# The low parts of the weights: GpSimd in quarters in the first layer, VectorE in the second

## The chip, the cores and the metric

The kernel runs on one core of one Trainium2 chip. The metric is the device time of one execution in microseconds (us). The engines are TensorE (PE; its weight loads are PEld), VectorE (DVE), ScalarE (ACT), GpSimd (POOL) and SyncE (SP), which here issues loads. Each engine works through its own instructions in the order of the program and waits for the others by semaphores.

## What is computed

```python
def reference(q, k, v, moe_*, moe2_*):
    x = attention(q, k, v)          # 4 x 8 heads, 576 tokens, window 32, plain or with dilation 4
    x = x as [2304, 512]
    # first layer: 8 experts with 288 tokens each; the largest logits of x @ w_gate choose first
    for e in range(8):
        out[mask_e] = relu(x[mask_e] @ w1[e]) @ w2[e]        # w1 [512, 1024], w2 [1024, 512]
    # second layer: each token goes to the two best experts of its noisy logits
    for e in range(8):
        out2[mask_e] += weight * (relu(x[mask_e] @ w1b[e]) @ w2b[e])
```

All inputs are float32, and the routing depends on small differences of the logits, so the products have to be nearly as exact as float32.

## The kernel before

The work has three parts: the attention (to about 104 us), the first layer with its routing (to about 500 us) and the second layer (to the end).

**Products in split form.** TensorE multiplies a shorter format (float32r) fast. So each operand is split into a high part, the number rounded to that format, and a low part, the rest; a product is the sum of high x high, high x low and low x high (`mm3`, L688). Weights come in chunks of 128 x 1024: four for an expert's first matrix, four for its second, 64 chunks in each layer. `split` (L662 to L668) makes the parts of one chunk: ScalarE copies `raw` into `whi` (L666), GpSimd subtracts `whi` from `raw` into `wlo` (L667). There are 10 buffers each for `whi` and `wlo` and 4 for `raw`; SyncE's loads run four chunks ahead.

```python
nc.scalar.activation(hi, raw, AF.Copy)
nc.gpsimd.tensor_tensor(lo, raw, hi.bitcast(F32), op=OP.subtract)
```

The other operands are split on ScalarE and VectorE: a token tile from PSUM into `xh` and `xl` (L671, L672), a hidden tile into `hh` and `hl` (L675, L676). The products write into four PSUM buffers `m`; one comes free when its `hl` is done.

**First layer.** `routing` finds, expert by expert, the threshold of the logits digit by digit. A round has three steps on VectorE and two on TensorE: VectorE compares (`I`, L479), TensorE counts (18 narrow products, L495), VectorE marks (`sat`, L497) and makes the next key ready (`wd`, L501), TensorE adds up (L506), VectorE takes the digit off (`w`, L510). `lister` then builds the list of the expert's tokens (L608 to L632), and GpSimd gathers their rows (`gather1`, L698). Between the routing's steps TensorE works on products of the expert before (`ffn1`).

**Between the layers** `noisy` (L804 to L849), `ranks0` and `ranks` work out the second layer's routing on VectorE.

**Second layer.** For each expert, `up` makes the first product on its 640 slots (segments of 256 and 384 columns) and `down` the second, 512 columns wide in five blocks, whose results GpSimd adds to the output rows (L1001). While an expert's first product runs, `slots` (L903 to L940) makes the next expert's list of tokens: VectorE's `rke` (L912), 24 one-hot blocks `R` (L917) and `A` (L924, L926), then 24 narrow products (L931).

**What sets the order.** The program is written out in the order in which it is to run. `build` keeps an estimated TensorE clock, `self.pe`, which each product moves on (`spend`), and puts routing steps, background tasks and splits among the products by it: `SPLITS1`, `SPLITS2` and `SPLITS2F` (L43 to L45) are the times, within an expert's products, at which the next chunk is split.

Of the kernel before, what the change touches and what calls it, by code (L numbers as in the profile page):

```python
# [22 lines left out]
CAP = N // E            # tokens of an expert of the first layer  # L23
NT = N // 128           # 18 token tiles
GB = 96                 # rows of a block of the first layer
NJ = CAP // GB          # 3 blocks
NCOL = E * NJ           # 24 columns of 96 positions
NA = NCOL - 2 * NJ      # those of all but the last two experts
XW = DM + E             # a gathered row: the token and its noise
CB = 5                  # blocks of 128 slots of an expert of the second layer  # L30
CAP2 = CB * 128
SEGS = ((0, 256), (256, 384))
BA = 3                  # blocks of the first expert that do not wait for the last of the first layer
SA = BA * 128
NB = 9                  # query blocks of 64
KW = 96                 # keys of a query block's window
DIGITS = (6, 6, 6, 7, 7)  # bits of the digits of a key
# [4 lines left out]
# times, in an expert's products, at which the next chunk of weights is split  # L42
# [4 lines left out]
LOAD = (3.0, 5.0)       # from a load's start to its arrival: of a known expert, of one that is read first  # L47
ROWS0 = (4, 1, 2, 1, 2, 1, 2, 1, 2, 1, 1)
WARM = (14, 2, 9)
HOP = (0.13, 0.2)       # from the vector to the tensor engine and back  # L50
SLACK = (0.1, 0.4, 0.0, 0.2)

# columns of the constants: those that stay, then those that are only converted
# [89 lines left out]
class Body:  # L143
# [3 lines left out]
    # ------------------------------------------------------------ constants  # L147
# [42 lines left out]
    # ------------------------------------------------------------ attention  # L190
    def attention(self, x0T):
        nc, tc, A = self.nc, self.tc, self.A
        with ExitStack() as ctx:
# [109 lines left out]
            def gate(b):  # L303
                """The four feature chunks' shares of the logits, each in a quarter of the partitions."""
                for o in (b * S, b * S + 288):
                    ps = pT.tile([128, 512], F32, name="ps")
                    for kk in range(4):
                        nc.tensor.matmul(ps[32 * kk:32 * kk + 32, :288], self.wg1[:, kk, :],
                                         x0T[kk][:, o:o + 288], start=True, stop=True)
                    nc.scalar.activation(gs[:, o:o + 288], ps[:, :288], AF.Copy)  # L310
# [15 lines left out]
            # the digits' values, by doubling  # L326
# [5 lines left out]
            def warm(n):  # L332
                """Keeps the tensor engine's clock up while it waits for loads."""
# [23 lines left out]
            for u, (g, j0, n) in enumerate(groups):  # L357
# [16 lines left out]
                if g == 4 and j0 == 0:  # L374
                    # the parts of the rows that the transpositions do not write
                    nc.sync.dma_start(self.xr[:, DM:XW], A["noise"])
                if CLEAR <= u < CLEAR + 9:
                    # zeros to which the second layer adds
# [6 lines left out]
    # ------------------------------------------------------- first routing  # L385
# [12 lines left out]
    def rows(self, x0T, c0, c1, psum, name, pool):  # L398
        """The tokens' rows of features for the gathers."""
# [9 lines left out]
    def routing(self):  # L409
        """Yields (kind, phase, time of the products that follow); an expert is closed in each phase."""  # L410
# [29 lines left out]
        def choices():  # L440
            """Each token's first best expert among the open ones, and order-preserving bits of its value."""
# [13 lines left out]
        def prefix():  # L455
            """Members of EQ before each, by columns."""
# [5 lines left out]
        def place(pk):  # L462
            """Ranks of the members; the others lie far behind."""
# [9 lines left out]
        for k in range(E - 1):  # L473
            ei = self.st.tile([1, 1], I32, name=f"ei{k}")
            self.EV[k] = ei
            # w: above, at or below the threshold's digits so far
# [54 lines left out]
            # the taken tokens leave  # L531
# [7 lines left out]
        # the expert that is left takes every token that has not been taken  # L539
# [24 lines left out]
    def chain(self, t):  # L564
        """The vector engine's time for the routing's next operations."""
# [3 lines left out]
    def shade(self, dur):  # L569
        """Work for the vector engine while the routing waits for products that take dur."""  # L570
# [7 lines left out]
    def later(self, t, f):  # L578
        """f as soon as the routing leaves the vector engine time for it."""
# [14 lines left out]
    def lister(self, k, rk):  # L594
        """The tokens of phase k's expert by their ranks, [96, 3], in pieces of work."""
# [45 lines left out]
    # ------------------------------------------------------------- weights  # L641
    def raw1(self, w1, c, e=None):
        """Rows 128c.. of an expert's first matrix, [512, 1024]."""
# [8 lines left out]
    def raw2(self, w2, c, e=None):  # L652
        """Rows 256c.. of an expert's second matrix, [1024, 512]."""
# [8 lines left out]
    def split(self, raw):  # L662
# [4 lines left out]
        nc.gpsimd.tensor_tensor(lo, raw, hi.bitcast(F32), op=OP.subtract)  # L667
        return hi, lo  # L668
# [10 lines left out]
    def mm3(self, ps, pairs, late=None):  # L679
        """ps = sum of a.T @ b over the pairs of split operands; yields its times."""  # L680
# [11 lines left out]
    # --------------------------------------------------------- first layer  # L692
# [26 lines left out]
    def ffn1(self, k):  # L719
        """Yields (unit name, time on the tensor engine)."""  # L720
# [4 lines left out]
        for f in range(8):  # L725
            ps = self.mm.tile([128, 512], F32, name="m")
            fs = slice(f * 128, (f + 1) * 128)
            yield from self.mm3(ps[:, :CAP], [((self.W[0, k, c][0][:, fs], self.W[0, k, c][1][:, fs]),
                                               (xh[:, c, :], xl[:, c, :])) for c in range(4)])
# [4 lines left out]
        for d in range(4):  # L734
            ps = self.mm.tile([128, 512], F32, name="m")
            pairs = []
            for f in range(8):
                c, a = divmod(f, 2)
                ds = slice(a * DM + d * 128, a * DM + (d + 1) * 128)
                pairs.append(((self.W[1, k, c][0][:, ds], self.W[1, k, c][1][:, ds]), (hh[:, f, :], hl[:, f, :])))  # L740
# [4 lines left out]
    def gate2(self, k):  # L745
        """Products with the second gate, by positions."""
# [16 lines left out]
    def rows1(self, k):  # L763
        """The rows of the first layer's output."""
# [582 lines left out]
```

## Time and profile before

| | us |
|---|---|
| median of 3 runs | 1029.07 |
| lowest and highest run | 1026.8, 1032.75 |
| the profiled execution (its span) | 1035.7 |
| PE, DVE, ACT, POOL busy in it | 944.6, 476.7, 368.5, 488.2 |
| mean granted TensorE clock | 0.905 of full |

The times of the profile are counted from the start of the span. A row of a timeline gives the start, the length, the engine, the line, the operation and the tiles (out<-in); in brackets stands the idle time ahead of it and what ended it. The granted clock is the one that the throttle gave TensorE; 1.0 is 2.4 GHz, 0.5 is 1.2 GHz.

### The profile page before, as it was taken

To read this page: it belongs to the slowest core of one execution; us is meant where nothing else is said; L and a number is where in the kernel's file an instruction comes from. 1 tells how busy PE (TensorE), PEld (TensorE's weight loads), DVE (VectorE), ACT (ScalarE), POOL (GpSimd) and SP (SyncE) were. 2 spreads that over 40 slices of the span, in tenths; PEclk is the share of its full clock that TensorE was granted. 3 is DMA by queue.
4 is the path that set the end of the run, shared out by engine and by line. 5 is a ranking of instruction groups with operands and counts; after the bars stand their busy time and mean duration, and the time that the engine had idled before them with its cause. 6 is when DMAs were issued, how large, how long until landed. Compare 5 with 4: busy or idle time off the path is not lost.

```text
span 1035.7 us, 17494 instructions
## 1 busy us (share of the span) xinstructions
PE 944.6 (91%) x6986; PEld 855.7 (83%) x6988; DVE 476.7 (46%) x1342; ACT 368.5 (36%) x669; POOL 488.2 (47%) x279
## 2 busy tenths in 40 slices
PE   8889947998989999996998989999898998989994
PEld 5677747988979989996997988988888898888983
DVE  6565476577375574238255460522616034160310
ACT  2657322232223234562551423423323343322310
POOL 4654045434425255774643665455454645545311
PEclk8989558788888689997999989999999999989998
DMA  9674452333313233562543445355353533533212
GB/s 301 204 244 140 184 186 87 100 111 99 109 61 121 90 105 126 189 207 84 157 144 72 127 139 132 82 139 97 101 122 92 152 74 113 104 112 92 28 18 38
DMA packets 59643, 126.33 MB, mean 122 GB/s; under 512 B 7456, under 2 KB 14880, under 8 KB 59552
## 3 DMA queue, kind: packets, MB, share of 16 engines
q1 hardware_dynamic: 46080, 94.50, 27.7%
q0 software_dynamic: 10496, 25.77, 13.2%
q10 hardware_dynamic: 2976, 4.85, 1.4%
q8 instruction: 57, 0.93, 0.4%
q14 instruction: 34, 0.28, 0.1%
HBM read 100.46 MB, written 24.72 MB: 121 GB/s over the span
## 4 chain that ended last, share of the span: by engine, by line
PE 70%; DVE 20%; DMA 4%; ACT 2%; issue 2%; POOL 1%; SPq 0%; ACTq 0%; POOLq 0%; DVEq 0%
PE m L688 53%; PE r L495 6%; DVE R L917 4%; DMA kt<-in_k_dram 2%; PE t L963 2%; PE s L236 2%; DVE hl L676 1%; PE o L287 1%; PE t L404 1%; DVE wd L501 1%; DVE rke L912 1%; PE t L712 1%; DMA out_dram<-y,tk 1%; DVE I L479 1%; PE ps L268 1%
## 5 line engine op out<-in xcount | busy, mean ns | idle before, releaser
L667 POOL TENSOR_TENSOR wlo<-raw,whi 128x1024 fp32r<-128x1024 f32 x128 | 319.4, 2513 | 275.0 <-ACT whi L666 261.3
L688 PE MATMUL m<-xh,whi 128*128 128x384 f32 (+2 forms) x768 | 248.0, 323 | 10.9 <-DVE hl L676 10.9
L688 PE MATMUL m<-xl,whi 128*128 128x384 f32 (+2 forms) x768 | 246.2, 321 | 0.0
L688 PE MATMUL m<-xh,wlo 128*128 128x384 f32 (+2 forms) x768 | 245.4, 320 | 0.0
L676 DVE SCALAR_TENSOR_TENSOR hl<-m,hh 128x256 fp32r<-128x256 f32 (+2 forms) x192 | 89.8, 474 | 191.3 <-ACT hh L675 191.2
L675 ACT ACTIVATE hh<-m 128x256 fp32r<-128x256 f32 (+2 forms) x192 | 82.0, 428 | 260.8 <-PE m L688 256.9
L688 PEld LDWEIGHTS m<-xh,whi 128*128 128x128 f32 x768 | 154.5, 201 | 13.0 <-DVE hl L676 12.6
L688 PEld LDWEIGHTS m<-xl,whi 128*128 128x128 f32 x768 | 154.8, 202 | 5.4 <-issue 5.0
L688 PEld LDWEIGHTS m<-xh,wlo 128*128 128x128 f32 x768 | 154.4, 201 | 0.5 <-POOL wlo L667 0.5
L666 ACT ACTIVATE whi<-raw 128x1024 fp32r<-128x1024 f32 x128 | 133.4, 1050 | 8.2 <-DMA raw<-in_w1a_dram 6.4
L688 PE MATMUL m<-whi,hl 128*128 128x512 f32 x320 | 126.0, 394 | 2.6 <-DVE hl L676 2.6
L688 PE MATMUL m<-whi,hh 128*128 128x512 f32 x320 | 128.3, 401 | 0.0
L1001 POOL DMA_INDIRECT out_dram<-y,tk x40 | 63.0, 1576 | 136.3 <-ACT y L1000 79.5
L688 PE MATMUL m<-wlo,hh 128*128 128x512 f32 x320 | 125.4, 392 | 0.0
L672 DVE TENSOR_TENSOR xl<-t,xh 128x512 fp32r<-128x512 f32 (+1 forms) x72 | 42.1, 586 | 169.0 <-ACT xh L671 168.8
L688 PE MATMUL m<-hh,whi 128*128 128x288 f32 x256 | 84.5, 330 | 3.4 <-DVE ge L608 3.4
L688 PE MATMUL m<-hl,whi 128*128 128x288 f32 x256 | 84.9, 332 | 0.0
L495 PEld LDWEIGHTS <-I 128*64 128x64 bf16 (+1 forms) x630 | 63.8, 195 | 25.1 <-DVE I L479 21.0
L688 PE MATMUL m<-hh,wlo 128*128 128x288 f32 x256 | 84.3, 329 | 0.0
L495 PE MATMUL r<-OH,I 128*64 128x8 bf16 (+1 forms) x630 | 66.8, 239 | 18.1 <-DVE I L479 18.1
L1000 ACT ACTIVATE y<-m,wte 128x512 f32<-128x512 f32 x40 | 27.6, 689 | 150.7 <-PE m L688 81.5
L688 PEld LDWEIGHTS m<-whi,hl 128*128 128x128 f32 x320 | 60.4, 189 | 16.1 <-DVE hl L676 3.5
(205 smaller groups left out, 1290.2 us busy)
## 6 DMA issues: line engine op xcount, KB each, us to landing
raw<-in_w1a_dram SPq DMA_DIRECT2D x32, 512.0 KB, 3.8
raw<-in_w2a_dram SPq DMA_DIRECT2D x32, 512.0 KB, 3.3
raw<-in_w1b_dram SPq DMA_DIRECT2D x32, 512.0 KB, 3.3
raw<-in_w2b_dram SPq DMA_DIRECT2D x32, 512.0 KB, 3.3
vt<-in_v_dram SPq DMA_DIRECT2D x8, 768.0 KB, 6.5
qt<-in_q_dram SPq DMA_DIRECT2D x8, 576.0 KB, 8.3
kt<-in_k_dram SPq DMA_DIRECT2D x8, 576.0 KB, 9.0
out_dram<-z SPq DMA_DIRECT2D x9, 512.0 KB, 7.4
```

Of the source, the lines that this page charges most:

```text
L236: nc.tensor.matmul(s[r, i, jj * KW:(jj + 1) * KW], QT[g][r, i, 64 * j:64 * j + 64], KT[g][r, i, w:w + KW], start=True, stop=True)
L495: nc.tensor.matmul(pc[:nb, :E], I[:, :nb, c], OH[:, c, :], start=c == 0, stop=c == NT - 1)
L666: nc.scalar.activation(hi, raw, AF.Copy)
L667: nc.gpsimd.tensor_tensor(lo, raw, hi.bitcast(F32), op=OP.subtract)
L672: self.nc.vector.tensor_tensor(xl, ps, xh.bitcast(F32), op=OP.subtract)
L675: self.nc.scalar.activation(hh, ps, AF.Relu)
L676: self.later(0.4, lambda: self.nc.vector.scalar_tensor_tensor(hl, ps, 0.0, hh.bitcast(F32), op0=OP.max, op1=OP.subtract))
L688: self.nc.tensor.matmul(ps, a, b, start=i == 0, stop=i == n - 1)
L917: V.tensor_scalar(R[:, c, :], self.iotab[:GB], rk[:, c:c + 1], None, op0=OP.is_equal)
L963: nc.tensor.transpose(ps[:, kk * 128:(kk + 1) * 128], g[:, kk * 128:(kk + 1) * 128], self.ident)
L1000: nc.scalar.activation(y, ps, AF.Copy, scale=wt[:, b:b + 1])
L1001: nc.gpsimd.indirect_dma_start(out=self.out, out_offset=bass.IndirectOffsetOnAxis(ap=tok[:, b:b + 1], axis=0), in_=y, in_offset=None, comp ...
```

## The change

In the first layer the low part of a chunk is still subtracted on GpSimd, in four instructions of 256 columns each. In the second layer it is subtracted on VectorE, in one instruction of 1024 columns. That one is not put into the program where the chunk is split, but kept (`pend`) until the estimated TensorE clock has moved on by 2.5, or until a product is about to use the chunk. TensorE's, ScalarE's and SyncE's instructions stay as they were, in the same order.

```diff
-    def split(self, raw):
+    def split(self, chunk, raw):
...
         nc.scalar.activation(hi, raw, AF.Copy)
-        nc.gpsimd.tensor_tensor(lo, raw, hi.bitcast(F32), op=OP.subtract)
-        return hi, lo
+        self.W[chunk] = hi, lo
+        if chunk[1] < E:
+            for q in range(0, F, F // 4):
+                s = slice(q, q + F // 4)
+                nc.gpsimd.tensor_tensor(lo[:, s], raw[:, s], hi[:, s].bitcast(F32), op=OP.subtract)
+        else:
+            self.pend[chunk] = self.pe + 2.5, lambda: nc.vector.tensor_tensor(lo, raw, hi.bitcast(F32), op=OP.subtract)
+
+    def lows(self, t=1e9):
+        for chunk in [c for c, (at, _) in self.pend.items() if at <= t]:
+            self.pend.pop(chunk)[1]()
+
+    def w(self, chunk, s):
...
+        if chunk in self.pend:
+            self.pend.pop(chunk)[1]()
+        hi, lo = self.W[chunk]
+        return hi[:, s], lo[:, s]
...
         def spend(t):
             self.pe += t
+            self.lows(self.pe)
...
-                self.W[chunks[i]] = self.split(raw[i])
+                self.split(chunks[i], raw[i])
```

`ffn1`, `up` and `down` take the parts of a chunk by `self.w(chunk, columns)` instead of from `self.W`.

VectorE, while an expert of the second layer makes its first product and the next expert's slots are worked out. Before (`rke`, `R` and `A` are tiles of `slots`, `hl` the low part of a hidden tile):

```order
L912 SCALAR_TENSOR_TENSOR rke<-a_7603,rke 96x24
L917 TENSOR_SCALAR R_7606<-iotab,rke 96x128 x6
L676 SCALAR_TENSOR_TENSOR hl_7481<-m,hh_7480 128x256
L917 TENSOR_SCALAR R_7606<-iotab,rke 96x128 x12
L676 SCALAR_TENSOR_TENSOR hl_7483<-m,hh_7482 128x384
L917 TENSOR_SCALAR R_7606<-iotab,rke 96x128 x6
L676 SCALAR_TENSOR_TENSOR hl_7481<-m,hh_7480 128x256
L921 TENSOR_TENSOR Ab_7678<-ge_7600 96x120
```

The same place in the change, whose lines from `split` on are numbered 18 or 19 higher:

```order
L930 SCALAR_TENSOR_TENSOR rke<-a_7794,rke 96x24
L935 TENSOR_SCALAR R_7797<-iotab,rke 96x128 x6
L695 SCALAR_TENSOR_TENSOR hl_7673<-m,hh_7672 128x256
L935 TENSOR_SCALAR R_7797<-iotab,rke 96x128 x6
L676 TENSOR_TENSOR wlo<-raw,whi 128x1024
L935 TENSOR_SCALAR R_7797<-iotab,rke 96x128 x6
L695 SCALAR_TENSOR_TENSOR hl_7675<-m,hh_7674 128x384
L935 TENSOR_SCALAR R_7797<-iotab,rke 96x128 x6
L695 SCALAR_TENSOR_TENSOR hl_7673<-m,hh_7672 128x256
L939 TENSOR_TENSOR Ab_7870<-ge_7791 96x120
```

One subtraction has come between the second and the third six of the 24 blocks `R`. The other seven of an expert lie outside these rows: two between the `hl` ahead of the slots, one behind the slots' results and four, in a row, ahead of the five `xl` of the next expert's tokens.

GpSimd, the first chunks of the first layer and the gathers of its first two experts. Before:

```order
L667 TENSOR_TENSOR wlo<-raw,whi 128x1024
L698 DMA g<-xr,idx_1888 96x520 x3
L667 TENSOR_TENSOR wlo<-raw,whi 128x1024 x11
L698 DMA g<-xr,idx_2448 96x520 x3
L667 TENSOR_TENSOR wlo<-raw,whi 128x1024 x5
```

In the change:

```order
L674 TENSOR_TENSOR wlo<-raw,whi 128x256 x4
L717 DMA g<-xr,idx_1891 96x520 x3
L674 TENSOR_TENSOR wlo<-raw,whi 128x256 x44
L717 DMA g<-xr,idx_2484 96x520 x3
L674 TENSOR_TENSOR wlo<-raw,whi 128x256 x20
```

Each subtraction has become four; the gathers stand at the same places among the chunks.

## Rows read from the trace of the kernel before

**Rows 1.** The source line L667: shortest, median and longest in ns; who waited (us, times).
```profile
L667 POOL TENSOR_TENSOR wlo<-raw,whi x128: 2330/2402/2998, 133.5 to 971.5; 128x1024 fp32r<-128x1024 f32 x128
...
  PEld m L688: 0.5, 1
```

**Rows 2.** The source lines L912 and L501, columns as in rows 1.
```profile
L912 DVE SCALAR_TENSOR_TENSOR rke<-a,rke x9: 174/2002/2002, 485.2 to 914.8; 96x24 f32<-96x24 f32 x8, 96x18 f32<-96x18 f32 x1
...
L501 DVE SCALAR_TENSOR_TENSOR wd<-w,dd x27: 162/166/6946, 111.2 to 364.9; 128x18 f32<-128x18 bf16 x27
```

**Rows 3.** Timeline of DVE around 668, within the first product of an expert.
```profile
664.81 0.56 DVE L676 SCALAR_TENSOR_TENSOR hl<-m,hh 128x384 fp32r<-128x384 f32 x1 [1.77 <-ACT hh L675]
...
666.24 2.00 DVE L912 SCALAR_TENSOR_TENSOR rke<-a,rke 96x24 f32<-96x24 f32 x1
668.27 1.06 DVE L917 TENSOR_SCALAR R<-iotab,rke 96x128 bf16<-96x128 bf16 x6
...
669.59 4.20 DVE L917 TENSOR_SCALAR R<-iotab,rke 96x128 bf16<-96x128 bf16 x12
```

**Rows 4.** Timeline of POOL in the same stretch.
```profile
665.80 2.40 POOL L667 TENSOR_TENSOR wlo<-raw,whi 128x1024 fp32r<-128x1024 f32 x1 [4.63 <-ACT whi L666]
```

**Rows 5.** Timeline of PE in the same stretch.
```profile
674.31 0.44 PE L688 MATMUL m<-xh,whi 128*128 128x384 f32 x1 [1.60 <-DVE hl L676]
...
677.01 0.76 PE L931 MATMUL r<-A,R 96*128 96x35 bf16 x24 [1.39 <-DVE A L926]
```

**Rows 6.** The chain that ended last: start, us, what; three of the experts.
```profile
677.77 30.00 PE m L688 x150
...
863.07 31.52 PE m L688 x150
...
926.49 32.19 PE m L688 x150
```

**Rows 7.** Stretches: length, busy PE, PEld, DVE, ACT, POOL; granted clock, DMA share, GB/s.
```profile
127.00:167.00 40.00, 19.79 (x147) 18.11 (x146) 30.16 (x62) 11.26 (x19) 22.28 (x11) 0.63 0.39 134
167.00:395.00 228.00, 216.74 (x1541) 201.69 (x1540) 145.85 (x448) 65.74 (x124) 92.92 (x47) 0.81 0.33 106
456.00:494.00 38.00, 28.89 (x203) 26.99 (x202) 31.33 (x130) 15.27 (x30) 19.65 (x10) 0.82 0.34 115
...
677.00:739.00 62.00, 59.00 (x366) 53.47 (x366) 21.98 (x58) 20.78 (x34) 32.06 (x18) 1.00 0.46 111
```

**Rows 8.** DVE by line and shape: count, busy us, mean ns, idle time before.
```profile
L672 DVE TENSOR_TENSOR xl<-t,xh 128x512 fp32r<-128x512 f32 x40 | 27.6, 691 | 157.7 <-ACT xh L671 157.7
...
L672 DVE TENSOR_TENSOR xl<-t,xh 128x288 fp32r<-128x288 f32 x32 | 14.4, 454 | 11.4 <-ACT xh L671 11.1
```

**Rows 9.** POOL by line and shape, columns as in rows 8.
```profile
L247 POOL TENSOR_TENSOR p<-p,mx 128x960 f32<-128x960 f32 x8 | 14.3, 1792 | 16.1 <-DVE mx L246 15.3 <-PE s L236 0.8
...
L247 POOL TENSOR_TENSOR p<-p,mx 128x768 f32<-128x768 f32 x8 | 11.8, 1470 | 3.1 <-DVE mx L246 2.7 <-PE o L287 0.4
```

**Rows 10.** Timelines of POOL, DVE and PE in the first expert's routing.
```profile
140.48 6.93 POOL L667 TENSOR_TENSOR wlo<-raw,whi 128x1024 fp32r<-128x1024 f32 x3
155.62 9.94 POOL L667 TENSOR_TENSOR wlo<-raw,whi 128x1024 fp32r<-128x1024 f32 x4 [8.21 <-ACT whi L666]
...
140.51 6.95 DVE L501 SCALAR_TENSOR_TENSOR wd<-w,dd 128x18 f32<-128x18 bf16 x1
...
161.28 2.02 DVE L510 TENSOR_SCALAR w<-wd,r 128x18 bf16<-128x18 f32 x1
163.34 3.44 DVE L479 TENSOR_TENSOR I<-thr,w 128x2304 bf16<-128x2304 bf16 x1
...
148.65 1.60 PE L495 MATMUL r<-OH,I 128*64 128x8 bf16 x12 [7.84 <-DVE I L479]
```

**Rows 11.** The chain that ended last: two of its stretched DVE pieces.
```profile
133.75 2.32 DVE dg L486 x2
...
386.75 2.80 DVE idx L631
```

More of the change, by code (lines that the diff above doesn't have):

```diff
@@ L727, in ffn1 @@
             fs = slice(f * 128, (f + 1) * 128)
-            yield from self.mm3(ps[:, :CAP], [((self.W[0, k, c][0][:, fs], self.W[0, k, c][1][:, fs]),
-                                               (xh[:, c, :], xl[:, c, :])) for c in range(4)])
+            yield from self.mm3(ps[:, :CAP], [(self.w((0, k, c), fs), (xh[:, c, :], xl[:, c, :])) for c in range(4)])
             self.split_h(ps[:, :CAP], hh[:, f, :], hl[:, f, :])
@@ L739, in ffn1 @@
                 ds = slice(a * DM + d * 128, a * DM + (d + 1) * 128)
-                pairs.append(((self.W[1, k, c][0][:, ds], self.W[1, k, c][1][:, ds]), (hh[:, f, :], hl[:, f, :])))
+                pairs.append((self.w((1, k, c), ds), (hh[:, f, :], hl[:, f, :])))
             yield from self.mm3(ps[:, :CAP], pairs, 5 if d == 0 else None)
@@ L978, in up @@
                 ps = self.mm.tile([128, 512], F32, name="m")
-                yield from self.mm3(ps[:, :n], [((self.W[0, E + e, c][0][:, fs], self.W[0, E + e, c][1][:, fs]),
-                                                 (xh[:, c, o:o + n], xl[:, c, o:o + n])) for c in range(4)])
+                yield from self.mm3(ps[:, :n], [(self.w((0, E + e, c), fs), (xh[:, c, o:o + n], xl[:, c, o:o + n])) for c in range(4)])
                 self.split_h(ps[:, :n], hh[:, f, :], hl[:, f, :])
@@ L996, in down @@
                 ds = slice(a * DM, (a + 1) * DM)
-                pairs.append(((hh[:, f, bs], hl[:, f, bs]), (self.W[1, E + e, c][0][:, ds], self.W[1, E + e, c][1][:, ds])))
+                pairs.append(((hh[:, f, bs], hl[:, f, bs]), self.w((1, E + e, c), ds)))
             yield from self.mm3(ps, pairs, 5 if b == b0 else None)
@@ L1024, in build @@
         nc.gpsimd.memset(self.cnt, 0.0)
-        self.G1, self.G2, self.X1T, self.XX, self.SL, self.HH, self.W = ({} for _ in range(7))
+        self.G1, self.G2, self.X1T, self.XX, self.SL, self.HH, self.W, self.pend = ({} for _ in range(8))
         self.pe = self.tR = self.dR = self.dv = self.rdy = 0.0
```

## The prediction

> **What bounds the kernel now.** I read the page first: TensorE is busy nine tenths of the span, VectorE and GpSimd less than half, so what can be won is TensorE's idle time behind the attention and the time it spends at its lower clock. Next I read the subtraction that is moved. On GpSimd it takes 2402 ns in the median, and TensorE waited for its result once, for 0.5 us [rows 1]. Its own length is hidden; what matters is what it does to others, and that shows on VectorE. The small instruction of L912 (96x24) takes 174 ns at best and 2002 ns in the median; that of L501 (128x18) takes 166 ns in the median and 6946 ns at worst [rows 2]. In the expert boundary that I looked at, L912 starts at 666.24 and ends at 668.24, just behind the GpSimd subtraction that began at 665.80 and ends at 668.20 [rows 3, 4]. The run of twelve L917 takes 4.20 us, though six take 1.06 [rows 3]; the next subtraction lies across it. So a VectorE instruction that reads two SBUF operands, or goes from SBUF to SBUF, stands still while GpSimd subtracts; those that read PSUM (L676, L672) are not stretched. **The wait for GpSimd to end ends last at these places**, though no semaphore carries it.
>
> TensorE pays for it. In this boundary it stood 1.60 us for an hl of L676, late behind the stretched L917, and 1.39 us for A of L926 [rows 5]: 3.0 us. The same pair stands in five experts (at 672.7, 734.5, 796.2, 858.0 and 921.3), and as much in the first boundary, at 606.6. Another stall stands ahead of 549. Behind some stalls the granted clock is the lower level: the 150 products behind the slots take 30.00 us in one expert, but 31.52 and 32.19 us in two others [rows 6], together 3.7 us more. In the first layer TensorE is idle for 40.00 - 19.79 = 20.2 us between 127 and 167, for 11.3 us between 167 and 395 and for 9.1 us between 456 and 494, at a mean granted clock of 0.63, 0.81 and 0.82 [rows 7].
>
> **The change, second layer.** 64 subtractions leave GpSimd; its gathers and scatters stay. VectorE gets 64. The trace has no such instruction on it; the nearest rows are L672, the same subtraction from PSUM: 691 ns for 512 columns, 454 for 288 [rows 8], so 1.06 ns a column and 149 fixed, **1.23 us** for 1024. The upper bound is GpSimd's 2.40, the lower 1.09, with nothing fixed. Eight per expert make 9.8 us more for VectorE, which was busy for 22 of 62 us [rows 7]. Four lie in the second product, where VectorE has only the five xl to do; two lie between hl, in its pauses, and one behind the slots' results. One lies within the slots, behind the second six of L917. It follows ScalarE's copy by several us, so it does not wait there. Queued behind it are two runs of L917, two hl and A.
>
> The slots' chain, from the hl ahead of it to A, took 12.2 us (664.81 to 677.01 [rows 3, 5]). The locks in it are 2.00 - 0.17 = 1.83 us at L912 and 4.20 - 2.12 = 2.08 us at L917. Less these and plus 1.23 it takes 9.5, and A ends at 674.3. Without the stall for hl (that hl then ends near 671.6, and was asked for at 672.7) TensorE would be there at 677.01 - 1.39 - 1.60 = 674.02 [rows 5]. So 0.3 of 3.0 us remain: 2.7 us for each of six boundaries, **16 us** (9 if one more subtraction falls into the chain, 18 at most). The longer products behind stalls give **3 us** (0 to 3.7). Around 549 two such waits go and up to four subtractions of 1.23 come into the same chain: **0** (-1 to 2).
>
> **The change, first layer.** 64 subtractions become 256. For the price of a quarter: GpSimd's subtractions of 960 and 768 columns take 1792 and 1470 ns [rows 9], so 182 ns are fixed; (2402 - 182) / 4 + 182 = **0.74 us**, at least 0.60 with nothing fixed. Four take 2.95, so a chunk holds GpSimd 0.55 us longer. These 64 x 0.55 = 35 us lie beside TensorE, whose products hardly wait for wlo [rows 1]; if that cover went, each chunk would come 0.55 us late.
>
> What VectorE wins depends on how it gets in. Between whole subtractions it does: GpSimd runs four from 155.62 to 165.56; w, begun at 161.28, ends at 163.30, and I goes from 163.34 to 166.78 [rows 10], held once by each of two subtractions. With quarters an instruction would wait 0.74 us at most instead of 2.4, but the next one may meet the next quarter. In the chain I count fifteen single waits between 133.75 and 386.75, the first and the last in [rows 11], whose instructions are 1.5 to 2.6 us longer than their like, 31 us in all. Bounds for each: 1.4 us won, if the other quarters run while VectorE waits for TensorE; 0.9 lost, if four quarters hit four instructions in turn. VectorE is idle for a good third of 167 to 395 [rows 7], so I take half of the win, 0.7: 10.5 us. The sixteenth wait is another. wd stood from 140.51 to 147.46, through three subtractions (140.48 to 147.41) right behind a gather, and TensorE stood 7.84 us [rows 10]; the last of the fifteen, L631, also began beside a gather and ended with the subtraction behind it. VectorE got in at no joint there. Twelve quarters would hold wd for 12 x 0.74 = 8.9 us, a loss of 1.9. Of 10.5 - 1.9 some 0.7 reaches TensorE (of its 31.5 us idle in 127 to 395 some 26 lie behind the first subtraction; the waits are 38): **6 us** (-11 to 19). In 456 to 494 six instructions were held about as long as L912, but there one instruction follows another without a pause, so each quarter would find a new one: **0** (-4 to 7). For the clock I take **2 us** (0 to 10): the first layer's narrow routing products precede most of its low stretches, and they stay.
>
> The row behind the gather is where the Trainium skill, page "SBUF — State Buffer", section "SBUF: two separate sides", speaks otherwise: the port pair that VectorE and GpSimd share is locked for one whole instruction by whichever begins first. By that rule wd would wait for one quarter and the sum be an estimated 6 us better; by the row it is not. The wait at L912 (2.0 us) agrees with the rule, the one through three subtractions does not.
>
> **Sum.** 16 + 3 + 0 + 6 + 0 + 2 = 27 us. The profiled execution took 1035.7, 6.6 above the median of the runs: 1035.7 - 27 = 1008.7 there, 1029.07 - 27 = **1002 us** for the median. The terms' bounds, added as squares since they go their own ways, are 17 us down and 19 up: 985 to 1021.
>
> **The rivals.**
> *Quarters hold the port as one piece.* If VectorE is let in at no joint between quarters, each of the fifteen waits grows by 0.55 and wd by 1.9, (8.3 + 1.9) x 0.7 = 7 us, and 456 to 494 loses 2 to 3; the second layer's 19 stay: 1029 - 19 + 10 = 1020. For it: wd and L631. Against it: w and I [rows 10]. Chance 0.18. The Trainium skill, page "GPSIMD Engine Reference", section "2.1 Instruction dispatch", has such a mechanism: each of GpSimd's cores goes on to the next instruction when its own share is done. The trace agrees behind gathers alone.
>
> *The subtraction takes the lock's place on VectorE.* If two more of the eight fall ahead of hl and A than the one I count, 1.23 each, the stalls of the second layer stay at 2.7, and only the first layer wins: 1029 - 8 = 1021. For it: VectorE would work some 22 of a first product's 28 us. Against it: the pauses ahead of each hl. That VectorE was not held by GpSimd at all, and the change only moves work, ends at the same place. Chance 0.10.
>
> *Quarters meet VectorE in turn: slower.* If GpSimd takes the port after each VectorE instruction and 2.5 quarters of each chunk hit one, VectorE waits 1.85 us per chunk, where it now waits 0.8 (38 and 12 us over 64 chunks): 64 x 1.05 x 0.7 = 47 us lost against 19 won, 1057. It decides from 64 x 0.7 x d = 19, d = 0.42 us more per chunk: 1.6 quarters. For it: w and I, held one behind the other. Against it: the third of its time in which VectorE waits for TensorE and quarters pass. Chance 0.07.
>
> *All joints free, and the clock with them.* Terms at their upper bounds: 18 + 4 + 2 + 19 + 7 + 10 = 60, 969. Chance 0.06.
>
> **How the numbers follow.** The forecast has the other 0.59. The range, 977 to 1021, holds nearly all of it and most of the first two rivals; the slower and the best case are left out. A measurement of this kernel tells about 0.5%, 5.1 us, from no change: faster is under 1023.9. Of the forecast, the best case and the first two rivals (0.93) I leave 0.07 for same: 0.86 faster, 0.07 same, 0.07 slower.
>
> **What would show it.** Second layer: L912 near 0.18 us, twelve L917 near 2.1 in sum, wlo on VectorE near 1.23 us, TensorE's stall ahead of L931 under 0.5 us, the 150 products 30.0 us in every expert. First layer: quarters of 0.60 to 0.74 us, single waits under 0.8 us, wd of the first expert held for 7 us or more. I am wrong if TensorE still stands 2 us at each expert boundary, if quarters take over 0.8 us, or if the 40 us of idle time between 127 and 494 grow.

## The result, and the profile after

| | before | the change |
|---|---|---|
| median of 4 runs, us | 1028.84 | 995.91 |
| lowest and highest, us | 1026.8, 1032.75 | 990.73, 1000.84 |
| span of the profiled run, us | 1035.7 | 988.9 |
| mean granted TensorE clock in it | 0.905 | 0.924 |

The ratio is 0.9659, with an interval of 0.9627 to 0.969: faster by 33 us, where 27 had been forecast. The spans of the two profiled runs lie on opposite sides of the medians (before 6.9 above, after 7.0 below) and differ by 46.8 us; terms that are read from the two profiles add up to that, not to 33.

The engines on the page of the change: GpSimd is busy for 376.6 us instead of 488.2, VectorE for 497.7 instead of 476.7.

```profile
PE 925.4 (94%) x6988; PEld 839.2 (85%) x6988; DVE 497.7 (50%) x1406; ACT 368.4 (37%) x669; POOL 376.6 (38%) x407
```

The source lines of the change that answer to [rows 1, 2] (shortest, median and longest in ns): the quarter on GpSimd, the subtraction on VectorE, `rke`, and `wd`.

```profile
L674 POOL TENSOR_TENSOR wlo<-raw,whi x256: 712/737/3000, 133.4 to 479.8; 128x256 fp32r<-128x256 f32 x128
...
L676 DVE TENSOR_TENSOR wlo<-raw,whi x64: 1211/1218/1228, 482.4 to 927.7; 128x1024 fp32r<-128x1024 f32 x64
...
L930 DVE SCALAR_TENSOR_TENSOR rke<-a,rke x9: 174/179/181, 465.0 to 873.2; 96x24 f32<-96x24 f32 x8, 96x18 f32<-96x18 f32 x1
...
L501 DVE SCALAR_TENSOR_TENSOR wd<-w,dd x27: 164/166/1669, 110.7 to 352.3; 128x18 f32<-128x18 bf16 x27
```

The two prices that no row of before had were right: 0.74 us a quarter (737 ns), 1.23 us the subtraction on VectorE (1218). `rke`, which took 2002 ns in the median, takes 179. The worst `wd` took 6946 ns and takes 1669.

**Second layer.** VectorE within one expert's first product, which answers to [rows 3]:

```profile
755.44 0.18 DVE L930 SCALAR_TENSOR_TENSOR rke<-a,rke 96x24 f32<-96x24 f32 x1
755.66 1.06 DVE L935 TENSOR_SCALAR R<-iotab,rke 96x128 bf16<-96x128 bf16 x6
...
757.94 1.22 DVE L676 TENSOR_TENSOR wlo<-raw,whi 128x1024 fp32r<-128x1024 f32 x1
...
762.71 0.60 DVE L944 TENSOR_TENSOR A<-Ab,W 96x360 bf16<-96x360 f32 x1
```

TensorE at the end of it, which answers to [rows 5]: the stall of 1.60 us for `hl` is gone, and of the 1.39 us for A 0.40 is left.

```profile
763.36 0.76 PE L949 MATMUL r<-A,R 96*128 96x35 bf16 x24 [0.40 <-DVE A L944]
```

In the chain that ended last, all six pieces of 150 products now take the time of the fast ones in [rows 6]; the first and the last of them:

```profile
587.38 30.00 PE m L707 x150
...
881.90 30.00 PE m L707 x150
```

**First layer.** The stretches of [rows 7] in the change. TensorE is idle for 11.4 us of the first (20.2 before), 10.3 of the second (11.3) and 6.3 of the third (9.1); the granted clock (before it the busy times) is 0.69, 0.84 and 0.91 instead of 0.63, 0.81 and 0.82.

```profile
127.00:167.00 40.00, 28.60 (x211) 26.37 (x211) 27.84 (x93) 12.43 (x22) 27.86 (x35) 0.69 0.45 151
167.00:395.00 228.00, 217.69 (x1587) 203.07 (x1588) 135.89 (x429) 72.49 (x138) 119.94 (x155) 0.84 0.33 108
456.00:494.00 38.00, 31.69 (x250) 30.16 (x249) 23.73 (x61) 16.39 (x27) 17.16 (x24) 0.91 0.48 156
```

These are the same times and not the same work: the first slots' product, in the third stretch, starts at 489.32 before and at 469.10 in the change. From 127 us to that product TensorE does the same 2310 products in both. It is idle meanwhile for 40.7 us before (362.30 - 321.59) and for 29.5 in the change, and busy for 9.0 us less (before, then the change):

```profile
127.00:489.30 362.30, 321.59 (x2310) 302.21 (x2310) 219.18 (x666) 124.03 (x232) 173.45 (x86) 0.82 0.37 121
```

```profile
127.00:469.10 342.10, 312.61 (x2310) 293.50 (x2310) 197.46 (x662) 123.74 (x231) 207.87 (x272) 0.85 0.39 128
```

The biggest single gain there contradicts the forecast. `wd` behind the first gathers was to be held through twelve quarters; the timelines of GpSimd, VectorE and TensorE, which answer to [rows 10], show it through in 0.28 us. TensorE's idle time of 7.84 us became 1.98.

```profile
139.97 8.85 POOL L674 TENSOR_TENSOR wlo<-raw,whi 128x256 fp32r<-128x256 f32 x12
...
139.86 0.28 DVE L501 SCALAR_TENSOR_TENSOR wd<-w,dd 128x18 f32<-128x18 bf16 x1
140.25 0.57 DVE L510 TENSOR_SCALAR w<-wd,r 128x18 bf16<-128x18 f32 x1
140.86 1.22 DVE L479 TENSOR_TENSOR I<-thr,w 128x1152 bf16<-128x1152 bf16 x1
...
142.13 1.12 PE L495 MATMUL r<-OH,I 128*64 128x8 bf16 x8 [1.98 <-DVE I L479]
```

Two things stayed as forecast. `idx`, behind another gather, is held through all four quarters that follow (GpSimd, then VectorE):

```profile
374.30 2.78 POOL L674 TENSOR_TENSOR wlo<-raw,whi 128x256 fp32r<-128x256 f32 x4
...
373.87 3.23 DVE L631 SCALAR_TENSOR_TENSOR idx<-cp 96x3 int32<-96x3 f32 x1
```

And where VectorE has one instruction behind the other, each meets a quarter of its own, so that TensorE's stall there is what it was (6.28 us before). VectorE, then TensorE:

```profile
457.08 0.72 DVE L861 CAST W<-nzs 96x144 bf16<-96x144 f32 x1
457.83 0.68 DVE L862 TENSOR_TENSOR nzs<-nzs,W 96x144 f32<-96x144 f32 x1
...
469.10 0.63 PE L949 MATMUL r<-A,R 96*128 96x21 bf16 x18 [6.31 <-DVE A L944]
```

### The profile page after: what moved, and what is told of

It is laid out like the page before. It is cut to its first block, busy times and chain, and to the rows that moved or that the text cites. A ratio compares the mean times of both kernels' runs of the same rounds, so it can differ in the third digit from the quotient of the medians.

```text
span 988.9 us, 17657 instructions
## 1 busy us (share of the span) xinstructions
PE 925.4 (94%) x6988; PEld 839.2 (85%) x6988; DVE 497.7 (50%) x1406; ACT 368.4 (37%) x669; POOL 376.6 (38%) x407
## 4 chain that ended last, share of the span: by engine, by line
PE 72%; DVE 18%; ACT 3%; issue 3%; DMA 2%; POOL 0%; SPq 0%; ACTq 0%; POOLq 0%; DVEq 0%
PE m L707 53%; PE r L495 6%; DVE R L935 3%; PE s L236 2%; PE t L981 2%; DVE hl L695 2%; DMA kt<-in_k_dram 1%; PE o L287 1%; PE t L404 1%; DVE wlo L676 1%; DVE I L479 1%; PE t L788 1%; PE t L731 1%; PE ps L268 1%; PE t L769 1%
## 5 line engine op out<-in xcount | busy, mean ns | idle before, releaser
L674 POOL TENSOR_TENSOR wlo<-raw,whi 128x256 fp32r<-128x256 f32 x256 | 190.2, 778 | 144.2 <-ACT whi L669 127.5
L707 PE MATMUL m<-xh,whi 128*128 128x384 f32 (+2 forms) x768 | 242.4, 316 | 1.2 <-DVE ge L608 1.2
L707 PE MATMUL m<-xl,whi 128*128 128x384 f32 (+2 forms) x768 | 242.5, 316 | 0.0
L707 PE MATMUL m<-xh,wlo 128*128 128x384 f32 (+2 forms) x768 | 241.1, 314 | 0.0
L1018 POOL DMA_INDIRECT out_dram<-y,tk x40 | 66.3, 1658 | 253.0 <-ACT y L1017 204.8
L707 PEld LDWEIGHTS m<-xl,whi 128*128 128x128 f32 x768 | 151.1, 197 | 4.6 <-issue 4.2
L707 PEld LDWEIGHTS m<-xh,whi 128*128 128x128 f32 x768 | 150.7, 196 | 3.2 <-DVE ge L608 1.5
L707 PEld LDWEIGHTS m<-xh,wlo 128*128 128x128 f32 x768 | 150.3, 196 | 0.5 <-issue 0.5
L669 ACT ACTIVATE whi<-raw 128x1024 fp32r<-128x1024 f32 x128 | 133.5, 1051 | 11.4 <-DMA raw<-in_w1a_dram 8.6
L676 DVE TENSOR_TENSOR wlo<-raw,whi 128x1024 fp32r<-128x1024 f32 x64 | 77.6, 1220 | 52.5 <-ACT whi L669 52.5
L967 POOL DMA_INDIRECT g<-x,pos x40 | 42.7, 1067 | 144.9 <-PE m L707 119.1
```

The costliest lines, as they stand in the source:

```text
L674: nc.gpsimd.tensor_tensor(lo[:, s], raw[:, s], hi[:, s].bitcast(F32), op=OP.subtract)
L676: self.pend[chunk] = self.pe + 2.5, lambda: nc.vector.tensor_tensor(lo, raw, hi.bitcast(F32), op=OP.subtract)
L707: self.nc.tensor.matmul(ps, a, b, start=i == 0, stop=i == n - 1)
L967: nc.gpsimd.indirect_dma_start(out=g[:, :DM], out_offset=None, in_=self.x1[:rows, :], in_offset=bass.IndirectOffsetOnAxis(ap=pos[:, b:b + ...
L1018: nc.gpsimd.indirect_dma_start(out=self.out, out_offset=bass.IndirectOffsetOnAxis(ap=tok[:, b:b + 1], axis=0), in_=y, in_offset=None, comp ...
```

## The experiments

Diffs are against the change, where nothing else is said; "quarters" are the four GpSimd instructions of a chunk.

### One layer alone

`e1_second_only` leaves the first layer's chunk whole on GpSimd:

```diff
-            for q in range(0, F, F // 4):
-                s = slice(q, q + F // 4)
+            for q in range(0, F, F // 1):
+                s = slice(q, q + F // 1)
                 nc.gpsimd.tensor_tensor(lo[:, s], raw[:, s], hi[:, s].bitcast(F32), op=OP.subtract)
```

> The first layer keeps its 64 whole subtractions on GpSimd; only the second layer's go to VectorE. Theory A (the two parts add up; GpSimd's subtraction holds VectorE's two-operand instructions, and taking it away frees the slots of each expert): the second layer's part alone, about 20 us of the 33, so 1005 to 1012 us; TensorE stands 0.5 us or less ahead of the slots' narrow products, and the first layer's waits stay as before (one of nearly 7 us behind the first gather). Theory B (most of the gain is the first layer's, since the routing sets when everything behind it starts): 1016 to 1024 us.

Measured: 1012.52 us, ratio 0.9779 (0.9736 to 0.9821), 22 us. That is theory A's mechanism, 0.5 us above its range, beside a kernel before that took 1034.95 us in these runs. The boundary has its rest of 0.41 us, and the first `wd` is held and TensorE idle as before:

```profile
141.51 6.95 DVE L501 SCALAR_TENSOR_TENSOR wd<-w,dd 128x18 f32<-128x18 bf16 x1
...
149.66 2.33 PE L495 MATMUL r<-OH,I 128*64 128x8 bf16 x18 [7.84 <-DVE I L479]
```

`e2_first_only` has the quarters in the first layer and the second layer's chunk whole on GpSimd:

```diff
-            self.pend[chunk] = self.pe + 2.5, lambda: nc.vector.tensor_tensor(lo, raw, hi.bitcast(F32), op=OP.subtract)
+            for q in range(0, F, F // 1):
+                s = slice(q, q + F // 1)
+                nc.gpsimd.tensor_tensor(lo[:, s], raw[:, s], hi[:, s].bitcast(F32), op=OP.subtract)
```

> The first layer's subtractions in quarters, the second layer's whole on GpSimd as before. Theory A: the first layer's part alone, 10 to 15 us, so 1014 to 1019 us, with 2 to 3 us of TensorE stall at each of six expert boundaries as before. Theory B: 1004 to 1012 us.

Measured: 1026.34 us, ratio 0.9921 (0.9885 to 0.9957), 8.6 us, less than either theory gave. The boundary has both stalls of before, as theory A had it:

```profile
661.25 0.44 PE L709 MATMUL m<-xh,whi 128*128 128x384 f32 x1 [1.61 <-DVE hl L697]
...
663.95 0.82 PE L951 MATMUL r<-A,R 96*128 96x35 bf16 x24 [1.39 <-DVE A L946]
```

So 2.2% and 0.8% stand against 3.4% for both; the parts add up within their intervals, and the second layer is about two thirds of it.

### Quarters in both layers

`e3_quarters_both` asks whether pieces would have done where the change moved the work away: the second layer's chunk goes to GpSimd in quarters too.

```diff
-            self.pend[chunk] = self.pe + 2.5, lambda: nc.vector.tensor_tensor(lo, raw, hi.bitcast(F32), op=OP.subtract)
+            for q in range(0, F, F // 4):
+                s = slice(q, q + F // 4)
+                nc.gpsimd.tensor_tensor(lo[:, s], raw[:, s], hi[:, s].bitcast(F32), op=OP.subtract)
```

> Quarters on GpSimd in both layers, nothing on VectorE. Theory A1 (after each quarter VectorE gets one instruction in, then the next quarter takes the port: a dense run of VectorE instructions meets all four quarters of a chunk): the slots are such a run, so their chain stays 3 to 6 us too long, TensorE stands 2 to 4 us at each boundary and the time is that of the first layer's part alone or worse, 1014 to 1024 us. Theory A2 (only the length of one GpSimd instruction matters; an instruction waits once and the rest run): the boundaries lose under 1 us each and the time is near the change's, 996 to 1003 us.

Measured: 1018.01 us, ratio 0.9827 (0.98 to 0.9854). Theory A1 holds: TensorE's two stalls at a boundary hardly move, 2.73 us in place of 2.99, and at the first boundary it stands longer than in `e2_first_only` (5.67 us here, 2.96 there):

```profile
596.98 0.58 PE L709 MATMUL m<-xh,whi 128*128 128x256 f32 x1 [5.67 <-DVE hl L697]
...
660.89 0.44 PE L709 MATMUL m<-xh,whi 128*128 128x384 f32 x1 [1.35 <-DVE hl L697]
...
663.59 0.76 PE L951 MATMUL r<-A,R 96*128 96x35 bf16 x24 [1.38 <-DVE A L946]
```

On VectorE `rke` takes 0.34 us there, but the six and twelve R behind it take 2.55 and 4.12 us, where 1.06 and 2.1 are free: in a dense chain quarters only move the waits. The median is 8.3 us below that of `e2_first_only`, the profiled span only 2.7, and that kernel's runs lie between 1018.84 and 1032.95. Five boundaries win 0.26 us each and the first loses more than that, so the difference of the medians is not shown to come from the boundaries; its cause stays open.

### The size of a piece

`e4_halves` and `e5_eighths` differ from the change in one number:

```diff
-            for q in range(0, F, F // 4):
-                s = slice(q, q + F // 4)
+            for q in range(0, F, F // 2):
+                s = slice(q, q + F // 2)
```

> As the change, but the first layer's chunks in two halves (about 1.29 us each by the fixed 0.18 us and 2.17 ns a column) instead of four quarters. If the single wait is what the first layer wins (at most one piece), halves win about two thirds of what quarters do: 998 to 1002 us. If it makes no difference how often VectorE is let in, halves give the change's time, 994 to 998; if what matters is GpSimd's sum per chunk (2.58 against 2.95 us), they are better, 992 to 995.

Measured: 998.71 us, ratio 0.9662 (0.9632 to 0.9692), not to be told from the change's. The first `wd` is held through six halves, and TensorE is idle for 8.26 us (GpSimd, VectorE, TensorE):

```profile
138.63 7.35 POOL L674 TENSOR_TENSOR wlo<-raw,whi 128x512 fp32r<-128x512 f32 x6
...
138.66 7.36 DVE L501 SCALAR_TENSOR_TENSOR wd<-w,dd 128x18 f32<-128x18 bf16 x1
...
147.22 2.33 PE L495 MATMUL r<-OH,I 128*64 128x8 bf16 x18 [8.26 <-DVE I L479]
```

In the change that stall was 1.98 us. Each of the two ratios has an interval of 3 us either way, which leaves room for some 4 us of the 6.3 between these stalls, so that halves are as good as quarters is not shown.

> The change with eighths of a chunk (128 columns) in place of quarters in the first layer. From halves (1.31 us, the change's ratio of 0.966) against quarters (0.74 us): Theory A, the size of a piece below a half hardly matters, since a single wait is already short and a dense run pays one piece each while GpSimd's work per chunk grows: an eighth takes 0.42 to 0.50 us, a chunk 3.5 to 4.0 us, single waits fall to under 0.5 us, total 993 to 999 us. Theory B, waits in proportion to the piece are what is left of the first layer's stalls: the idle time of 6.31 us falls by 2 us or more and the total to 988 to 992 us. Theory C, GpSimd, now 1 us slower per chunk, comes late with low parts: TensorE waits for wlo from GpSimd, total 1003 us or more.

Measured: 1010.1 us, ratio 0.981 (0.9773 to 0.9848), 1.5% worse than quarters. The price of a piece was right (456 ns in the median), and none of the three theories has the reason: no low part came late, but VectorE was kept out of whole runs of eighths, 10.24 us of one instruction behind the gathers at 140 and 12.03 us of another at 448.43, which made TensorE stand 8.76 us. There too a gather's instruction stands right ahead of the run of eighths: it ends at 446.91, the run begins at 446.93 (GpSimd, VectorE, TensorE):

```profile
445.99 0.92 POOL L717 DMA_INDIRECT g<-xr,idx  x1 [0.30 <-PE m L707]
446.93 13.36 POOL L674 TENSOR_TENSOR wlo<-raw,whi 128x128 fp32r<-128x128 f32 x32
...
448.43 12.03 DVE L825 TENSOR_TENSOR nzs<-nzs,nz 96x144 f32<-96x144 f32 x1
...
462.56 0.61 PE L707 MATMUL m<-hh,whi 128*128 128x288 f32 x1 [8.76 <-DVE hl L695]
```

So the forecast's first rival, pieces that hold VectorE out as one, is what eighths do behind these gathers. An eighth came every 13.36 / 32 = 0.42 us, so some 28 joints between instructions passed before VectorE got in. The Trainium skill, page "SBUF — State Buffer", section "SBUF: two separate sides", gives the port pair that the two engines share to one of them for one whole instruction. The trace does not agree: by that rule VectorE would have waited for one eighth, not for 28.

### Why the first `wd` got in

`e7_first_whole` is the change with the very first chunk whole, so that routing and gathers stand to each other as in the kernel before:

```diff
+            n = F if chunk == (0, 0, 0) else F // 4
-            for q in range(0, F, F // 4):
-                s = slice(q, q + F // 4)
+            for q in range(0, F, n):
+                s = slice(q, q + n)
```

> The change, but the very first chunk (first matrix of the first expert, the subtraction that ends at 136 us) in one piece on GpSimd; all else as in the change. Question: why the first wd behind the gathers is let in at 0.28 us in the change, where it was held 6.95 us before. Theory A, timing: in the change the gathers start some 0.1 to 0.2 us later against the routing, so wd starts (139.86 us) before the first quarter that is queued behind the third gather (139.97); with the first chunk whole the routing and the gathers stand as before, wd starts about 0.03 us behind that quarter and is held until twelve quarters are done: wd 8 to 9 us, TensorE idle 9 to 10 us there, total 1000 to 1006 us. Theory B, the joints between quarters let wd in behind a gather too: wd at most 0.8 us, TensorE idle 2 to 3 us there, total within 3 us of the change (995.9).

Measured: 992.66 us, ratio 0.9617 (0.9573 to 0.966). Theory A falls. `wd` starts 0.03 us behind the quarter, just as it started 0.03 us behind the whole subtraction before [rows 10], and is through in 0.17 us (GpSimd, VectorE):

```profile
141.56 8.86 POOL L675 TENSOR_TENSOR wlo<-raw,whi 128x256 fp32r<-128x256 f32 x12
...
141.59 0.17 DVE L501 SCALAR_TENSOR_TENSOR wd<-w,dd 128x18 f32<-128x18 bf16 x1
```

Its number is theory B's, but B does not hold as a rule either: halves and eighths have joints and held VectorE at this place, and quarters held `idx` at 373.87. Nor is it the same from one execution to the next: in `e10_change_again`, the change once more, `wd` starts 0.05 us behind the quarter and takes 1.49 us, through two quarters, and TensorE stands 3.19 us. What lets VectorE in stays open.

### The last chunks, and the whole first layer, on VectorE

`e8_last_vector` takes the second matrix of the first layer's last expert off GpSimd:

```diff
-        if chunk[1] < E:
+        if chunk[1] < E and chunk[:2] != (1, E - 1):
```

> The change, but the four chunks of the last first-layer expert's second matrix (the sixteen quarters from 453.1 to 464.7 us, beside the noisy logits and the first ranks) subtracted on VectorE behind ScalarE's copy too. Theory A, the dense run of VectorE there takes a quarter's length per instruction because the two engines take turns: without the quarters its instructions take 0.15 to 0.4 us instead of 0.6 to 0.93, the run ends some 6 us earlier, TensorE's idle time of 6.31 us before the first slots' product (line 949) falls to 0 to 2 us, and the total to 989 to 993 us. Theory B, that wait is the length of VectorE's own chain, or the four subtractions put on VectorE (4 x 1.22 us) fill what is freed: idle 4 to 7 us, total 994 to 998 us.

Measured: 991.46 us, ratio 0.9639 (0.9608 to 0.9671), not to be told from the change. The expectation had the wrong chunks: only eight of the sixteen quarters beside the noisy logits were that matrix's. TensorE's stall is 4.05 us instead of 6.31; the small instructions behind the last quarter take 0.17 to 0.23 us, those beside quarters 0.7 as before. The direction is theory A's, half of its size.

`e6_vector_both` puts all low parts on VectorE:

```diff
-        if chunk[1] < E:
-            for q in range(0, F, F // 4):
-                s = slice(q, q + F // 4)
-                nc.gpsimd.tensor_tensor(lo[:, s], raw[:, s], hi[:, s].bitcast(F32), op=OP.subtract)
-        else:
-            self.pend[chunk] = self.pe + 2.5, lambda: nc.vector.tensor_tensor(lo, raw, hi.bitcast(F32), op=OP.subtract)
+        self.pend[chunk] = self.pe + 2.5, lambda: nc.vector.tensor_tensor(lo, raw, hi.bitcast(F32), op=OP.subtract)
```

> The change with the first layer's low parts on VectorE too: GpSimd subtracts nothing any more and holds nothing. Theory A, VectorE's order costs in the first layer what the port no longer does: between 127 and 167 us, where the routing bounds, seven to nine subtractions of 1.22 us stand in VectorE's order ahead of the routing's next instructions (9 to 11 us, less 3 to 5 of waits that go), and later each one that falls into a chain of the routing that is waited for adds its 1.22 us: total 997 to 1008 us. Theory B, with no piece of GpSimd left, what remains of the first layer's stalls goes (the 6.31 us, single waits of up to 0.74 us): total 983 to 992 us.

Measured: 982.59 us, ratio 0.9529 (0.9489 to 0.9569): theory A falls, and the time is just under B's range. The subtractions do stand ahead of the routing, four in a row at 149.04, but TensorE pays 1.18 us for those and 2.92 us for the next three; between 127 and 167 us it is idle for 12.1 us, at a lower granted clock (0.54, the change 0.69), between 167 and 395 for 1.0 us (the change: 11.4 and 10.3). The stretches:

```profile
127.00:167.00 40.00, 27.94 (x175) 24.11 (x174) 25.72 (x82) 12.59 (x20) 3.37 (x3) 0.54 0.40 136
167.00:395.00 228.00, 227.03 (x1680) 213.32 (x1680) 153.51 (x499) 76.56 (x145) 23.90 (x20) 0.85 0.38 121
```

The stall at the first slots' product, which quarters could not move, falls from 6.31 to 1.42 us with no GpSimd beside that chain:

```profile
461.71 0.60 PE L944 MATMUL r<-A,R 96*128 96x21 bf16 x18 [1.42 <-DVE A L939]
```

The gathers of the first layer are still there, and the longest `wd` takes 175 ns and the longest `idx` 159: without subtractions behind them the gathers held neither.

### What a place in VectorE's order costs

`e9_none_in_slots` takes `e6_vector_both` and keeps pending low parts back while the slots are built:

```diff
     def lows(self, t=1e9):
+        if self.held:
+            return
...
+        self.held = True
         R = wk.tile([GB, NCOL, 128], BF, name="R2", tag="R")
...
                         self.W3[:, :n, e:e + 1, :].to_broadcast([GB, n, nb, 3]), op=OP.mult)
+        self.held = False
         yield 0.0, 3.0
...
+        self.held = False
```

> All low parts on VectorE in both layers, and none of them while VectorE builds an expert's slots (from the first of the rows R to the last product with the weights): the one subtraction of 1.22 us that stands there is issued behind them. Theory A, VectorE's chain to the slots' product ends last at each of the six boundaries by 0.40 to 0.41 us, and without the 1.22 us it ends first: those idle times go, 6 x 0.4 us, and perhaps one of 1.28 us at the second expert; total 978 to 981 us against the 982.6 of all low parts on VectorE. Theory B, TensorE there waits for its own load of the slots' rows or for an earlier product, not for VectorE: the idle times stay and the total is within 1 us of 982.6. Theory C, a low part that is put off is then late for the first product of the next expert: idle times of 1 us or more at products with wlo, total 985 us or more.

Measured: 976.72 us, ratio 0.9466 (0.9429 to 0.9504), 1.3 us below theory A's range. Its mechanism holds: the product at the boundary has no idle time ahead of it any more, and the subtraction stands behind A (TensorE, VectorE). From one run of 150 products to the next it takes 58.36 us, where `e6_vector_both` takes 58.91. The intervals of the two ratios overlap, so the medians alone do not show how much it wins.

```profile
577.86 0.77 PE L948 MATMUL r<-A,R 96*128 96x35 bf16 x24
...
576.63 0.61 DVE L942 TENSOR_TENSOR A<-Ab,W 96x360 bf16<-96x360 f32 x1
577.13 1.21 DVE L671 TENSOR_TENSOR wlo<-raw,whi 128x1024 fp32r<-128x1024 f32 x1
```

`e10_change_again` is the change once more, beside `e9_none_in_slots` on the same chip.

> The change itself once more, on the chip of these runs, so that versions can be set against it: 0.963 to 0.969 of the kernel before, as measured first.

Measured: 993.04 us, ratio 0.964 (0.9591 to 0.9689). `e9_none_in_slots` beats it by 16 us, and both kernels of this case.

`e11_twice` is the change with each of the second layer's subtractions done twice, one behind the other.

```diff
+            def sub():
+                nc.vector.tensor_tensor(lo, raw, hi.bitcast(F32), op=OP.subtract)
+                nc.vector.tensor_tensor(lo, raw, hi.bitcast(F32), op=OP.subtract)
-            self.pend[chunk] = self.pe + 2.5, lambda: nc.vector.tensor_tensor(lo, raw, hi.bitcast(F32), op=OP.subtract)
+            self.pend[chunk] = self.pe + 2.5, sub
```

> The change, with each of the second layer's subtractions done twice on VectorE (64 more of 1.22 us, 78 us of VectorE's time; the result is the same). What does VectorE's time cost there? Theory A, only what stands in the chain that TensorE waits for: one subtraction per boundary lies among the rows of the slots, so that the idle time of 0.41 us becomes about 1.6 us at six boundaries and nothing else moves: 7 to 9 us more than the change. Theory B, VectorE's order holds up the products' hidden parts too (hl behind two subtractions): TensorE waits at products as well, 15 us or more above the change. Theory C, it all lies in slack: within 2 us of the change.

Measured: 1012.11 us, ratio 0.9819 (0.9778 to 0.986), 19 us above the change: theory B's number. The boundary alone is as theory A had it, 1.38 us instead of 0.40. The two profiled spans differ by 18.4 us. About half of that, 9.3 us, lies ahead of the first run of 150 products (596.66, in the change 587.38); there an `hl` now holds TensorE around 530 us. The other 9.3 us lie between the first and the last of these runs (303.85 us, in the change 294.52): 6.4 at five boundaries, and 2.9 because two of the runs are longer, 31.52 and 31.40 us.

```profile
529.53 0.50 PE L710 MATMUL m<-whi,hl 128*128 128x512 f32 x1 [2.03 <-DVE hl L698]
...
534.66 0.75 PE L952 MATMUL r<-A,R 96*128 96x14 bf16 x24 [2.54 <-DVE A L947]
...
595.91 0.76 PE L952 MATMUL r<-A,R 96*128 96x35 bf16 x24 [1.38 <-DVE A L947]
...
717.02 31.52 PE m L710 x150
```

## Why the prediction was right, and where its steps failed

**What bounds.** Right: the wait for GpSimd's subtraction, which no semaphore shows, was what TensorE paid for. In the second layer `e1_second_only` takes the stalls away and `e2_first_only` has them again. In the first, `e6_vector_both` is idle for 18.2 us from 127 us to the first slots' product (461.71), where it was 40.7 before and 29.5 in the change. Taken off GpSimd altogether, the subtraction gives the best kernels here.

**Second layer, 16 us at the boundaries.** Right. The rest was to be 0.3 us and is 0.40; 2.99 - 0.40 = 2.6 at a boundary where 2.7 was forecast. The second rival's mechanism is real and costs more than its place there: `e11_twice` adds one subtraction to the chain, the boundary's stall grows by 1.0 us, 6 us in all, but the total by 19, since the chain around 530 and longer products pay as well.

**Second layer, 0 around 549.** Right in TensorE's idle time: the stall of 2.60 us ahead of 549.00 gave way to 1.28 and 0.75. The stalls of over 0.4 us on TensorE between 490 and 612, before:

```profile
549.00 0.80 PE L688 MATMUL m<-whi,hl 128*128 128x512 f32 x1 [2.60 <-DVE hl L676]
...
608.94 0.39 PE L688 MATMUL m<-xh,whi 128*128 128x256 f32 x1 [2.30 <-DVE hl L676]
...
611.36 0.69 PE L688 MATMUL m<-xh,whi 128*128 128x384 f32 x1 [0.60 <-DVE hl L676]
```

and in the change:

```profile
528.81 0.75 PE L949 MATMUL r<-A,R 96*128 96x14 bf16 x24 [1.28 <-DVE A L944]
...
557.86 0.63 PE L981 MATMUL t<-ct,g 128*128 128x128 f32 x4 [0.75 <-DMA g<-x,pos]
```

**Second layer, clock 3 us.** Too small: this is the term that was mis-sized. From the first slots' product to the end TensorE does the same 3107 products in both. It is idle meanwhile for 34.8 us before and 18.4 in the change, 16.4 less, which is the 16 + 0 of the forecast. But it is also busy for 511.57 and 501.27 us, 10.3 less for the same products, at a mean granted clock of 0.97 and 0.99 (before, then the change; the clock stands behind the busy times).

```profile
489.30:1035.70 546.40, 511.57 (x3107) 463.56 (x3106) 185.25 (x536) 180.54 (x299) 260.58 (x146) 0.97 0.41 101
```

```profile
469.10:988.80 519.70, 501.27 (x3107) 455.72 (x3106) 227.36 (x600) 180.62 (x299) 114.64 (x88) 0.99 0.42 106
```

Between the two kernels with one half each the difference is 7 us: `e2_first_only`, with the second layer of before, is busy for 509.02 us over these products, `e1_second_only` for 502.00. So some 7 to 10 us came with the clock where 3 (at most 3.7) were taken. The forecast had counted the longer products of two experts alone; the 150 products at 614.93 took 31.06 us as well. In all this half was forecast at 19 us, and `e1_second_only` measured 22.

**First layer, 6 + 2 us.** The sum of 8 fits `e2_first_only` (8.6 us, by its interval 4.5 to 11.9), but its parts do not, so that it fits is partly luck. The step that failed is "twelve quarters would hold wd, a loss of 1.9": the stall behind it fell by 5.9 us (7.84 to 1.98). The fifteen single waits then gave less than the 10.5 x 0.7 = 7.4 us that were taken: TensorE's idle time between 127 and 395 fell by 9.8 us in all (8.8 + 1.0), so 3.9 beside `wd`. The clock is the least certain term, forecast at 2 (0 to 10): over the 2310 products up to the first slots' product TensorE is busy for 9.0 us less in the change's profile, but for only 3.5 less in that of `e2_first_only` (318.12 us). The signs that the forecast had named for this layer came half true: quarters took 0.74 us, but single waits reached 3.23 us (`idx`) and 1.67 us (`wd`), and the first expert's `wd` was not held for 7 us or more.

**The range.** The bounds that were added up gave 985 to 1021, while the range is stated as 977 to 1021. The measured 995.91 lies in both.

**The dense run in 456 to 494, 0 us.** Right, for the reason given: 6.28 us before, 6.31 after, and 1.42 with GpSimd idle.

**The first rival**, quarters that hold the port as one piece, was given 0.18. With quarters it holds behind some gathers; with eighths it holds behind three, for 5 to 12 us, and costs 1.5%. The forecast was not far from it: that a joint lets VectorE in is not what these runs show behind a gather. **The third rival**, quarters in turn, is what a dense chain shows (0.7 us an instruction), but only there, and there the stall stayed as it was (6.28 and 6.31 us).

## What to carry to other kernels

When small instructions of one engine take ten times their usual length with no semaphore behind it, look for an instruction of another engine that ends at the same moment, and price the move of that work by its length on the waiting engine (1.22 us for 2.40). Here moving it away won more than cutting it up: quarters in the first layer won about 1%, VectorE in their place another 1.3%. A chain without pauses meets one piece per instruction, and eighths were worse than quarters. Once it is moved, its place in the order counts too: one subtraction of 1.22 us, issued behind the awaited chain instead of within it, took 0.4 us of idle time from each of six boundaries.

## What was not expected of the hardware

- Joints between GpSimd's subtractions let VectorE in or not, and no run shows what decides it. With the same lag of 0.03 to 0.05 us, `wd` was held through 3 whole subtractions (6.95 us, in two kernels) and 6 halves (7.36 us), but took 0.17 to 1.49 us beside quarters. The long waits have one thing in common: in all the traces nine waits of VectorE go through several pieces and last over 3 us (3.23 to 12.03 us), and each lies in a run of pieces that begins within 0.03 us of the end of a gather's instruction on GpSimd. Other such runs let VectorE in, so a gather ahead is not enough, and no run takes the gathers away from the subtractions. The Trainium skill, page "GPSIMD Engine Reference", section "2.1 Instruction dispatch", says that each of GpSimd's cores takes the next instruction by itself; that would leave the port no common gap, but no run here tests it.
- Behind like stalls TensorE's clock fell or did not: in `e11_twice` boundaries with stalls of 1.38 to 1.39 us were followed by 150 products of 29.99 to 30.00 us in four experts and of 31.52 and 31.40 in two, at a mean granted clock of 0.95 instead of 1.00; in the change, with 0.40 us, all six took 30.0. The size of the stall alone does not tell which.
